# Forward substitution over two 32-token blocks in place of a 64-token block inverse, in a delta-rule attention and gated-convolution kernel

## The chip, the cores and the metric

The kernel runs on one core of one Trainium2 chip. The metric is the time of one execution on the device in microseconds (us); a lower time is better. Engines are named as in the profile: TensorE (PE, with its weight loads as PEld), VectorE (DVE), ScalarE (ACT), GpSimd (POOL) and the queue that issues the transfers (SP).

## The reference, cut to what matters

```
# q, k, v: (4 batches, 8 heads, 768 tokens, 48), beta: (4, 8, 768), all float32
k_n = k / (norm(k) + 1e-6)
state = 0                                  # (4, 8, 48, 48)
for t in range(768):
    y[t]  = q[t] @ state                   # read before the update
    v_old = k_n[t] @ state
    state = state + beta[t] * outer(k_n[t], v[t] - v_old)
x = y, heads side by side                  # (4, 768, 384)
gate_pre[t] = sum over j < 5 of conv_w[j] * x[t - 4 + j]   # per channel
out = (sigmoid(gate_pre) * (x @ w_val)) @ w_out
```

The weights w_val, conv_w and w_out arrive as 64-bit floats and are converted on the chip. All products are float32; in the trace each float32 matmul appears as two MATMUL records and two weight loads.

## The kernel before, in words

The 768 tokens are cut into 12 chunks of 64; a chunk is two blocks of T = 32 tokens. Two chunks make a group, so there are 6 groups. A "unit" is one batch and head; there are 32, worked side by side in the four 32-partition strips and along the free axis.

**prep(g)**, once a group, needs no state. `gram` multiplies keys by keys and by queries (k k' and k q'), `gk` (ScalarE) copies the key part out of PSUM to GD, and `ga` (VectorE, L494) masks the query part into AQ. On VectorE `trans_in` (L523) transposes the 32 by 32 diagonal blocks, `coef` (17 small steps) finds the norms, and then each 32 by 32 triangular block is inverted: `row` (L564, L566) makes 8 by 8 inverses, `mergez8` and `merget8` (L580 to L595) make 16 by 16 ones, `zmul`, `zred`, `tmul`, `tred` (L599 to L619) make 32 by 32 ones. The result is transposed twice, `trans_t` (L623) and `trans_n` (L626). In group 0 alone (FAST) the last merge is made by TensorE instead (`p1`, `p2`, `p3`, with copies). Then `bd0`, `lev1`, `zevac`, `lev2`, `tevac` join the two 32-token inverses of a chunk to one 64-token inverse BD: `lev1` (L686) and `lev2` (L697) are 32 by 32 products on TensorE, with narrow copies by ScalarE. `vscale` (ScalarE) scales the values by the norms.

**chain(c)**, once a chunk, is the serial part: `estep` (keys times state, L801), `esum` (VectorE, L805, subtracts the values), `ustep` (BD times that, L812), `uevac` (three ScalarE copies to US), `sstep` (adds to the state in PSUM, L822), `sevac` (copies it out for the next chunk). `qstep` (L833) and `ystep` (L841) make the output, `flip` (L851) transposes it.

**moe(c)** is the gated convolution: `conv` (L892) makes the first nt taps of the convolution with TensorE, `tap` (L898) the other 5 - nt with VectorE, `sig` (ScalarE), `val` (L907), `gate` (L910), `outp` (L915), `oevac`. nt is 2 for chunks 0 to 5 and 1 for 6 to 11.

Loads go through one queue, each held back until the second load before it has landed. The order of all instructions is made when the kernel is built: a planner simulates the five engines with listed costs, ranks and biases, takes the highest rank among what is ready, chooses the PSUM bank, and puts in `keep_warm` matmuls on zeros (L958) where TensorE would stand idle. Each engine then runs its own list in that order.

Of the kernel before, what the change touches and what calls it, by code (L numbers as in the profile page):

```python
# [21 lines left out]
KW = 5 * T  # L22
# [4 lines left out]
BIAS = {  # L27
    'LB': -1138.3, ('LB', 0): 7.4, 'LK0': 530.9, ('LK0', 0): -481.0, 'LKQ': 1110.0, ('LKQ', 0): -19.7,
    ('LKQ', 1): 156.3, ('LKQ', 2): 217.7, ('LKQ', 3): -442.9, ('LKQ', 4): -892.6, ('LKQ', 5): -89.1, 'LKT': -576.7,
    ('LKT', 0): -196.1, ('LKT', 1): -334.4, ('LKT', 2): 445.2, ('LKT', 3): -254.0, ('LKT', 4): 323.2,  # L30
# [4 lines left out]
    'coef': 468.0, ('coef', 0): 263.6, ('coef', 1): -4.1, ('coef', 2): -237.8, ('coef', 3): -109.9, ('coef', 4): 84.2,  # L35
    ('coef', 5): -151.7, 'const': 613.2, ('const', 0): 1209.5, 'conv': 28.7, ('conv', 0): -1.9, ('conv', 1): -155.4,
    ('conv', 2): 135.3, ('conv', 3): 335.1, ('conv', 4): -180.2, ('conv', 5): 605.0, 'cscale': -43.3,
    ('cscale', 0): -117.7, ('cscale', 1): -746.4, ('cscale', 2): -14.6, ('cscale', 3): 116.5, ('cscale', 4): 29.6,
    ('cscale', 5): -381.6, 'diag': 1076.5, ('diag', 0): -1247.6, 'estep': -7.9, ('estep', 0): 288.5,
    ('estep', 1): -5.2, ('estep', 2): -41.9, ('estep', 3): 734.0, ('estep', 4): 74.9, ('estep', 5): -89.3,  # L40
    'esum': -83.1, ('esum', 0): -380.5, ('esum', 1): -432.1, ('esum', 2): 323.2, ('esum', 3): 833.7,
    ('esum', 4): 122.3, ('esum', 5): 282.5, 'eye': -40.5, ('eye', 0): -581.3, 'f64_bits': 179.7,
    ('f64_bits', 0): -110.7, 'f64_join': -266.8, ('f64_join', 0): -364.4, 'f64_low': 270.2, ('f64_low', 0): 791.0,
    'flip': 208.0, ('flip', 0): 127.2, ('flip', 1): -93.2, ('flip', 2): 82.9, ('flip', 3): 292.3, ('flip', 4): -243.4,
    ('flip', 5): 174.0, 'ga': 126.9, 'gate': -104.8, ('gate', 0): -759.9, ('gate', 1): 509.6, ('gate', 2): -463.4,
# [3 lines left out]
    ('gramK', 0): 128.0, 'gramQ': 430.1, ('gramQ', 0): -160.4, ('gram', 1): -704.8, ('gram', 2): -104.0,  # L49
    ('gram', 3): -4.8, ('gram', 4): 563.1, ('gram', 5): 99.1, 'halo': 185.7, ('halo', 0): -312.1, ('halo', 1): -20.4,  # L50
    ('halo', 2): 245.9, ('halo', 3): -202.4, ('halo', 4): 460.8, ('halo', 5): -382.3, 'high': 162.3, 'lev1': 80.3,
# [6 lines left out]
    ('norm', 1): 328.3, ('norm', 2): -366.6, ('norm', 3): 266.0, ('norm', 4): 610.1, ('norm', 5): -506.2,  # L58
    'oevac': -1050.8, ('oevac', 0): -639.5, ('oevac', 1): 223.7, ('oevac', 2): -293.3, ('oevac', 3): -491.9,
    ('oevac', 4): 428.8, ('oevac', 5): 997.7, 'ones': -1017.8, ('ones', 0): -412.1, 'outp': 254.2,  # L60
    ('outp', 0): -290.2, ('outp', 1): -378.5, ('outp', 2): 246.7, ('outp', 3): 155.7, ('outp', 4): 185.1,
    ('outp', 5): 238.1, 'p1': -8.9, ('p1', 0): -189.4, 'p2': -61.8, 'p2evac': -59.9, ('p2evac', 0): 440.8,
    ('p2', 0): -32.9, 'p3': 33.8, 'p3evac': 482.3, ('p3evac', 0): 751.7, ('p3', 0): -185.1, 'pack': -348.7,
    ('pack', 0): 465.1, 'qstep': 59.2, ('qstep', 0): 391.9, ('qstep', 1): 424.1, ('qstep', 2): -186.8,
    ('qstep', 3): -217.3, ('qstep', 4): -80.2, ('qstep', 5): -107.5, 'row': -870.9, ('row', 0): 33.6,
    ('row', 1): -118.1, ('row', 2): -337.1, ('row', 3): 162.6, ('row', 4): 31.4, ('row', 5): -725.8, 'sevac': 686.4,
    ('sevac', 0): 379.9, ('sevac', 1): -1074.3, ('sevac', 2): 1019.5, ('sevac', 3): 811.9, ('sevac', 4): 1118.8,
    ('sevac', 5): -215.4, 'sig': -419.1, ('sig', 0): 468.8, ('sig', 1): -444.3, ('sig', 2): 787.5, ('sig', 3): -763.0,
    ('sig', 4): 169.1, ('sig', 5): 290.8, 'small': 629.3, ('small', 0): 122.8, 'split': -143.9, ('split', 0): 337.1,
# [944 lines left out]
```

## Time and profile before

| | |
|---|---|
| median of 3 runs | 339.22 us (338.83 to 339.41) |
| profiled execution, span | 340.4 us, mean granted TensorE clock 0.910 |
| TensorE busy | 294.2 us (86%), weight loads 236.6 us |
| VectorE busy | 265.4 us (78%) |
| ScalarE busy | 195.9 us (58%) |
| GpSimd busy | 17.6 us (5%) |
| TensorE matmul records | 8370, 214 of them keep_warm |
| moved by transfers | 34.58 MB |

The profiled execution gives no time beside its span; the span is 1.2 us above the median of the runs. Busy times say how much of the span an engine had an instruction in flight. Records of small matmuls overlap, so what a product costs TensorE is read from start to start in the timeline, not from the mean duration of a record.

### The profile page before, as it was taken

What the parts mean: (1) busy time and instruction counts of PE and PEld (TensorE: products, weight loads), DVE (VectorE), ACT (ScalarE), POOL (GpSimd) and SP (SyncE); (2) the same over time, 40 slices, a digit from 0 to 9 for tenths busy, and PEclk for the clock granted to TensorE, in tenths of its full rate; (3) what the DMA queues carried; (4) which work ended last, traced back from release to release, by engine and by line L of the source; (5) the groups of instructions that cost most, each with busy time, mean ns of one, the idle gap of its engine ahead of it and who ended that gap; (6) DMA issues with size and microseconds to landing.
All of it is one profiled execution on the core that took longest, in us unless ns stands there. A gap on an engine that the chain in (4) does not pass through costs nothing.

```text
span 340.4 us, 18482 instructions
## 1 busy us (share of the span) xinstructions
PE 294.2 (86%) x8370; PEld 236.6 (70%) x8370; DVE 265.4 (78%) x655; ACT 195.9 (58%) x569; POOL 17.6 (5%) x31
## 2 busy tenths in 40 slices
PE   5898544977859898988996997998999999999994
PEld 4797544876647776875875885877866787687862
DVE  5569869895257999998999866999999899827430
ACT  4211759999545965357955478616599351873321
POOL 0000022322200000000000000000000000000000
PEclk9589855969678999999999589999999999999999
DMA  4885666131612527060147104345221301300213
GB/s 149 271 251 155 193 187 187 52 91 58 202 53 81 171 54 233 19 196 11 50 81 257 58 4 157 62 125 162 58 65 26 98 4 25 73 4 2 49 23 69
DMA packets 12379, 34.58 MB, mean 102 GB/s; under 512 B 1933, under 2 KB 5133, under 8 KB 12301
## 3 DMA queue, kind: packets, MB, share of 16 engines
q1 hardware_dynamic: 12300, 33.41, 33.4%
q8 instruction: 65, 1.06, 1.3%
q14 instruction: 14, 0.11, 0.1%
HBM read 28.69 MB, written 4.72 MB: 98 GB/s over the span
## 4 chain that ended last, share of the span: by engine, by line
PE 45%; DVE 21%; ACT 15%; issue 10%; DMA 7%; SPq 0%; POOL 0%; DVEq 0%; ACTq 0%
PE PB L907 8%; PE SPS L958 6%; PE PB L915 5%; PE PB L892 5%; ACT VN L348 5%; PE PB L484 5%; DMA KQ<-in_kq_dram 5%; DVE GT L898 4%; PE PB L801 2%; ACT BD L348 2%; PE PB L833 2%; DVE ZT L606 2%; ACT US L348 2%; DVE PR L599 2%; PE PB L851 2%
## 5 line engine op out<-in xcount | busy, mean ns | idle before, releaser
L907 PE MATMUL PB<-X,WV 128*128 128x256 f32 x216 | 52.5, 388 | 1.5 <-DVE GT L910 1.0
L915 PE MATMUL PB<-WO,GT 128*128 128x384 f32 x144 | 50.6, 495 | 0.1
L348 ACT ACTIVATE VN<-VN,NRM 128x48 f32<-128x48 f32 x192 | 45.1, 326 | 2.2 <-DMA PACE<-VN 2.0
L907 PEld LDWEIGHTS PB<-X,WV 128*128 128x128 f32 x216 | 39.8, 191 | 8.5 <-DVE GT L910 1.2
L898 DVE SCALAR_TENSOR_TENSOR GT<-X,CW,GT 128x256 f32<-128x256 f32 x90 | 38.7, 478 | 0.1
L958 PE MATMUL SPS<-ZW 128*128 128x128 f32 x214 | 35.1, 319 | 3.0 <-DVE SPS L400 2.8
L915 PEld LDWEIGHTS PB<-WO,GT 128*128 128x128 f32 x144 | 26.3, 190 | 15.5 <-DVE GT L910 0.3
L484 PE MATMUL PB<-KQ 48*32 48x96 f32 (+2 forms) x1536 | 26.6, 263 | 11.7 <-issue 9.2
L958 PEld LDWEIGHTS SPS<-ZW 128*128 128x128 f32 x214 | 31.2, 224 | 4.4 <-DVE SPS L400 2.8
L484 PEld LDWEIGHTS PB<-KQ 48*32 48x32 f32 x1536 | 21.3, 113 | 16.0 <-issue 11.9
L892 PE MATMUL PB<-X,CD 128*128 128x256 f32 x108 | 32.0, 432 | 0.1
L348 ACT ACTIVATE OS<-PB 128x384 f32<-128x384 f32 x24 | 11.6, 487 | 34.4 <-PE PB L915 33.1
L910 DVE TENSOR_TENSOR GT<-PB,GT 128x256 f32<-128x256 f32 x36 | 14.9, 417 | 20.5 <-PE PB L907 20.5
L494 DVE TENSOR_TENSOR AQ<-PB,MASK 128x256 f32<-128x256 f32 x48 | 19.2, 418 | 12.7 <-ACT GD L348 12.6
L898 DVE SCALAR_TENSOR_TENSOR GT<-X,CW,PB 128x256 f32<-128x256 f32 x36 | 16.6, 475 | 13.8 <-PE PB L892 8.7
L348 ACT ACTIVATE US<-PB 64x384 f32<-64x384 f32 (+1 forms) x36 | 17.5, 486 | 16.8 <-PE PB L812 9.2
L348 ACT ACTIVATE GD<-PB 128x256 f32<-128x256 f32 x48 | 15.6, 381 | 18.8 <-PE PB L484 18.4
L348 ACT ACTIVATE BD<-PB 32x256 f32<-32x256 f32 (+1 forms) x50 | 19.1, 383 | 8.7 <-PE PB L697 5.8
L892 PEld LDWEIGHTS PB<-X,CD 128*128 128x128 f32 x108 | 21.0, 210 | 3.6 <-DVE GT L898 0.3
L902 ACT ACTIVATE GT<-GT 128x256 f32<-128x256 f32 x36 | 13.6, 413 | 15.3 <-DVE GT L898 15.2
L841 PEld LDWEIGHTS PB<-US,AQ 64*64 64x64 f32 x768 | 14.3, 146 | 9.7 <-ACT US L348 7.1
L348 ACT ACTIVATE ZS<-PB 32x256 f32<-32x256 f32 x48 | 17.9, 373 | 4.1 <-PE PB L686 3.1
(117 smaller groups left out, 481.9 us busy)
## 6 DMA issues: line engine op xcount, KB each, us to landing
KQ<-in_kq_dram SPq DMA_DIRECT2D x24, 640.0 KB, 5.0
VN<-in_vt_dram SPq DMA_DIRECT2D x12, 384.0 KB, 3.5
KT<-in_kt_dram SPq DMA_DIRECT2D x12, 384.0 KB, 3.2
out_dram<-OS SPq DMA_DIRECT2D x48, 96.0 KB, 2.2
BD<-in_k_dram SPq DMA_DIRECT2D x2, 512.0 KB
OS<-in_w_val_dram SPq DMA_DIRECT2D x2, 384.0 KB, 4.0
GT<-in_w_out_dram SPq DMA_DIRECT2D x2, 384.0 KB
PACE<-KQ SPq DMA_DIRECT2D x24, 0.0 KB
```

The source lines that it names most:

```text
L348: A.activation(out=out, in_=in_, func=AF.Copy, **kw)
L484: PE.matmul(o, w, y, start=True, stop=True, tile_position=(64 * r, q))
L494: V.tensor_tensor(out=AQ[c % NAQ][:, r, 4 * i:4 * i + 4, :].rearrange("p h (n t) -> p h n t", t=T), in0=gview(c, i, r, part)[:, :, 0:3:2, ...
L599: V.tensor_tensor(out=PR[:, 0:64 * n].rearrange("p (k i j) -> p k i j", k=4, i=16), op=ALU.mult, in0=tl4[:, 1, :, 0, 4 * kb:16].unsqueeze( ...
L841: PE.matmul(bank("y", c, r)[a:a + C, D * h:D * h + D], aq[64 * t:64 * t + C, r, h, :], us[64 * t:64 * t + C, r, h, :], start=c == 0 and h ...
L892: PE.matmul(p, CD[:, m, k], x[:, m, :, k:k + C], start=(k == 0), stop=(k == nt - 1))
L898: V.scalar_tensor_tensor(out=GT[m], in0=x[:, m, :, k:k + C], scalar=CW[:, m, k:k + 1], in1=csum(m) if k == nt else GT[m], op0=ALU.mult, op ...
L902: A.activation(out=GT[m], in_=csum(m) if nt == KS else GT[m], func=AF.Sigmoid)
L907: PE.matmul(p, WV[:, k, 128 * m:128 * m + 128], xs[:, k], start=(k == 0), stop=(k == NKX - 1))
L910: V.tensor_tensor(out=GT[m], in0=bank("v", c, m)[:, 0:B * C].rearrange("p (b t) -> p b t", t=C), in1=GT[m], op=ALU.mult)
L915: PE.matmul(bank("o", c, i)[:, 0:DM], GT[k][:, 2 * i:2 * i + 2, :].rearrange("p b t -> p (b t)"), WO[:, k, :], start=(k == 0), stop=(k == ...
L958: PE.matmul(SPS[0][:, 384:512], ZW, ZW, start=False, stop=True, skip_group_check=True)
```

## The change: what it does

The 64-token inverse is no longer built. BD keeps only the 32 by 32 inverses (in another layout, read with a stride), and the chain solves the chunk in two steps: `ustep(0)` applies the inverse to the first block, two copies bring the result out, `ucross` multiplies it by the key products between the two blocks and adds that onto what `estep` left in PSUM for the second block, `esum(1)`, `ustep(1)` and two more copies finish it. `estep` is issued as 64 matmuls of 32 columns instead of 32 of 64. `lev1`, `lev2`, `bd0`, `zevac`, `tevac` and `trans_n` go.

FAST is empty: group 0 uses VectorE's `zmul` to `tred` as the others do, and `p1` to `p3` are never called. `gram` becomes one 64 by 128 product per unit (32 matmuls per chunk instead of 64); in groups 1 to 5 GpSimd then puts the blocks in place (`gmove`, 4 copies of 32 partitions a chunk). In group 0 keys are multiplied first (`gram0`), half of the copies out are VectorE's (`gkv`). `coef` has 15 steps instead of 17. GpSimd also copies norms (`nswap`) and does one step of the weight conversion. The convolution taps on TensorE become 3 for chunks 0 to 3, 1 for 4 to 7 and 0 for 8 to 11. Keys and queries are loaded as two tensors without the copies that were in `kq`: a half chunk has 512 KB instead of 640 KB, and the separate key load of group 0 is the first half itself. PSUM banks are cleared at the start by VectorE and ScalarE. The planner is gone: ORDER lists the number of each operation in the order of issue (-1 is a `keep_warm`), and SLOTS the PSUM banks.

```diff
+WG = 544
+FAST = ()
+NTAP = [3, 3, 3, 3, 1, 1, 1, 1, 0, 0, 0, 0]
+F64P = (1,)
+ORDER = [
+    13, 12, 20, 1, 0, 2, 3, -1, 5, -1, 4, 14, 6, 17, 15, 135, 21, 18, 19, 16, 301, 24, 8, 22, 23, 300, -1, 25, 26,
...
+]
...
+    V.memset(SPS[0], 0.0)
+    for i in range(NBANK):
+        if i < 3:
+            V.memset(PB[i], 0.0)
+        else:
+            copy(PB[i], ZW[:, 0:1].to_broadcast([128, 512]))
...
 def gram(c, i, part):
+            for r, t in STREAMS:
+                rows = slice(64 * r, 64 * r + D)
+                w = x[rows, 0, t ^ r, h, :]
+                o = bank("g", c, i, r, part)[64 * t:64 * t + C]
...
+                    PE.matmul(o[:, 2 * C * j:2 * C * j + 2 * C].rearrange("p (n e) -> p n e", e=C), w, x[rows, :, t ^ r, h, :],
+                              start=True, stop=True, tile_position=(64 * r, 64 * t))
...
+    def gmove(c, r, t):
+        u = unit(c // 2, c, r)[64 * t + T * (1 - r):64 * t + T * (1 - r) + T].rearrange("p h (n e) -> p h n e", e=T)
+        G.tensor_copy(out=u[:, :, r], in_=u[:, :, 1 - r])
...
+        def trans_t(i):
+            V.transpose(out=BD[gb][:, 16 * i:16 * i + 16], in_=tf[:, :, 16 * i:16 * i + 16].rearrange("p k j -> p j k"))
...
         def estep():
             for h in range(H):
+                for s in range(2):
+                    for r, t in STREAMS:
+                        q = 64 * t + T * s
+                        PE.matmul(bank("e", c, r ^ s)[q:q + T, D * h:D * h + D], x[64 * r:64 * r + D, 0, t ^ r, h, T * s:T * s + T],
+                                  sp[64 * r:64 * r + D, t ^ r, h, :], start=h == 0, stop=not s ^ r, skip_group_check=True,
+                                  tile_position=(64 * r, q))
+        def ustep(n):
+            for h in range(H):
                 for r, t in STREAMS:
+                    q = 64 * t + T * (r ^ n)
+                    PE.matmul(bank("u", c, r)[q:q + T, D * h:D * h + D], bd[q:q + T, :, u0 + 8 * r + h],
+                              (E2 if n else E1 if c else vn[:, 0])[q:q + T, h, :], start=True, stop=True, tile_position=(q, q))
+        def ucross():
+            for h in range(H):
+                for r, t in STREAMS:
+                    q, to = 64 * t + T * r, 64 * t + T * (1 - r)
+                    PE.matmul(bank("e", c, 1)[to:to + T, D * h:D * h + D], unit(g, c, r)[q:q + T, h, T * (1 - r):T * (1 - r) + T],
+                              us[q:q + T, r, h, :], start=c == 0 and h == 0, stop=True, skip_group_check=True, tile_position=(q, to))
...
+        add("PE", ustep, (0,), w=both("up"), take=both("u"), r=["E1" if c else ("VN", 0, 0), ("BD", g % 2, c % 2)])
+        for r in range(2):
+            add("ACT", uevac, (r,), r=[("up", c, r)], w=[("U", c % 2, r)])
+        add("PE", ucross, r=Ur + GDL, w=[("ep", c, 1)], take=() if c else [("e", c, 1)])
+        add("DVE", esum, (1,), r=[("ep", c, 1)] + VS[1], w=["E2"], give=[("e", c, 1)])
+        add("PE", ustep, (1,), w=both("up"), r=["E2", "q", ("BD", g % 2, c % 2)])
```

Numbering the operations as the changed file adds them gives 1,528. Read with that numbering, ORDER has 159 `keep_warm` entries, 153 of them ahead of chunk 2's `estep`; it puts 99 VectorE instructions from group 0's first `trans_in` up to chunk 0's `ustep(0)` and 178 up to chunk 2's `estep`; between that `estep` and the last `trans_t` of group 5 it has 405 VectorE instructions, and behind that point TensorE has, as the bulk, 7 `outp` and 9 `val`. In the stretches around a chain it puts one `val`, `outp` or `conv` between `ustep(0)` and `ucross`, and mostly one between `ucross` and `ustep(1)`.

## Rows read from the trace of the kernel before

**Rows 1.** Four stretches: busy time of each engine (instructions), clock, DMA.
```profile
0.00:66.70 66.70, 47.00 (x1760) 42.95 (x1760) 51.66 (x166) 34.80 (x103) 7.51 (x14) 0.77 0.60 181
66.70:106.20 39.50, 30.37 (x1123) 25.60 (x1122) 21.93 (x45) 27.18 (x76) 7.31 (x9) 0.74 0.30 93
106.20:291.00 184.80, 172.63 (x4654) 134.47 (x4653) 170.59 (x397) 113.14 (x341) 2.54 (x8) 0.97 0.32 93
291.00:341.00 50.00, 44.19 (x846) 33.61 (x844) 21.18 (x49) 20.78 (x50) 0.22 (x1) 1.00 0.15 34
```

**Rows 2.** Timeline of TensorE: start, length, count of records.
```profile
66.66 1.61 PE L812 MATMUL PB<-VN,BD 64*64 64x48 f32 x64
...
106.16 1.15 PE L801 MATMUL PB<-ST,KQ 48*64 48x48 f32 x64
```

**Rows 3.** Timeline of VectorE: start, length.
```profile
9.93 1.91 DVE L523 STREAM_TRANSPOSE TLP<-GD 128x1024 f32<-128x1024 f32 x1 [3.24 <-ACT GD L348]
...
57.27 1.58 DVE L599 TENSOR_TENSOR PR<-TLP,TT__78 128x768 f32<-128x768 f32 x1
...
289.02 2.22 DVE L623 STREAM_TRANSPOSE BD<-TT__78 128x1024 f32<-128x1024 f32 x1
```

**Rows 4.** VectorE by line, 106.2 to 341 us: count, busy us, mean ns.
```profile
L898 DVE SCALAR_TENSOR_TENSOR GT<-X,CW,GT 128x256 f32<-128x256 f32 x87 | 37.2, 478 | 0.0
...
L612 DVE TENSOR_TENSOR PR<-ZT,TR 128x256 f32<-128x256 f32 (+3 forms) x16 | 13.1, 821 | 0.3
...
L606 DVE TENSOR_REDUCE ZT<-PR 128x64 f32<-128x1024 f32 (+3 forms) x16 | 13.0, 814 | 0.3
...
L494 DVE TENSOR_TENSOR AQ<-PB,MASK 128x256 f32<-128x256 f32 x24 | 9.7, 420 | 0.3 <-ACT GD L348 0.3
L623 DVE STREAM_TRANSPOSE BD<-TT__78 128x1024 f32<-128x1024 f32 x4 | 8.9, 2218 | 0.0
L626 DVE STREAM_TRANSPOSE TNA<-TT__78 128x1024 f32<-128x1024 f32 x4 | 7.9, 1969 | 0.0
L564 DVE TENSOR_TENSOR PR<-TT__78,TLP 128x16 f32<-128x16 f32 (+5 forms) x24 | 6.1, 254 | 0.7
...
L580 DVE TENSOR_TENSOR PR<-TLP,TT__78 128x256 f32<-128x256 f32 (+1 forms) x16 | 5.0, 354 | 0.2
...
L584 DVE TENSOR_REDUCE ZT<-PR 128x64 f32<-128x512 f32 (+1 forms) x8 | 4.4, 553 | 0.3
...
L536 DVE SCALAR_TENSOR_TENSOR QUOT<-QUOT,SQ 128x32 f32<-128x32 f32 x10 | 1.9, 189 | 0.1
```

**Rows 5.** One weight-conversion step, whole trace by form.
```profile
L429 DVE TENSOR_SCALAR GT<-GT 128x384 uint32<-128x384 uint32 x3 | 1.1, 354 | 0.0
```

**Rows 6.** Timeline of TensorE from 213.9 us, full clock.
```profile
213.90 1.88 PE L484 MATMUL PB<-KQ 48*32 48x96 f32 x128
215.70 2.86 PE L907 MATMUL PB<-X,WV 128*128 128x256 f32 x12
218.49 0.94 PE L822 MATMUL SPS<-US,KT 64*48 64x48 f32 x64
219.36 0.87 PE L851 MATMUL PB<-EYE,YS 128*128 128x128 f32 x6
220.07 2.10 PE L915 MATMUL PB<-WO,GT 128*128 128x384 f32 x6
222.10 1.15 PE L801 MATMUL PB<-ST,KQ 48*64 48x48 f32 x64
223.18 1.56 PE L892 MATMUL PB<-X,CD 128*128 128x256 f32 x6
```

**Rows 7.** Timeline of TensorE: a 32 by 32 product.
```profile
244.71 1.31 PE L686 MATMUL PB<-BD,GD 32*32 32x32 f32 x128
```

**Rows 8.** ScalarE by line and form: one copy of the chain.
```profile
L348 ACT ACTIVATE US<-PB 128x384 f32<-128x384 f32 x12 | 5.9, 489 | 16.3 <-PE PB L812 9.2 <-DVE GT L898 7.0
```

**Rows 9.** Timeline of GpSimd: two weight joins of one size.
```profile
57.04 0.99 POOL L441 TENSOR_TENSOR WV<-WV,GT 128x384 f32<-128x384 f32 x1 [11.40 <-ACT WV L437]
58.11 1.59 POOL L442 TENSOR_TENSOR WV<-WV,GT 128x384 f32<-128x384 f32 x1
```

More of the change, by code (lines that the diff above doesn't have):

```diff
@@ L1 @@
-import math
 from contextlib import ExitStack
@@ L141, in add @@
             self.bank[key] = n
+            self.slot[key] = len(self.slot)
         for key in give:
             first = self.bank[key]
[L144 to L145 removed]
+            self.ops[first][3].update(d for d in deps if d < first)
+        self.ops.append((eng, fn, args, deps, tuple(take), tuple(give)))
         self.kinds.append((kind or fn.__name__, self.part))
@@ L263, with where @@
+        seen = set()
+        for n in ORDER:
+            if n >= 0:
+                assert self.ops[n][3] <= seen
+                seen.add(n)
+        assert len(seen) == len(self.ops)
+        return ORDER
+    def where(self, key):
+        return SLOTS[self.slot[key]]
 @with_exitstack
@@ L713, in plan_gram @@
             for i in range(2):
                 gg = [("g", c, i, r, part) for r in range(2)]
-                add("PE", cost, gram, (c, i, part), cols=cols, size=128, r=use, w=[("gp", c, i, r, part) for r in range(2)],
-                    take=gg, kind="gram" + part)
+                gp = [("gp", c, i, r, part) for r in range(2)]
+                if part == "K":
+                    add("PE", gram0, (c, i), r=[K], w=gp, take=gg)
+                else:
+                    add("PE", gram, (c, i, part), r=[K, ("KQ", c % NKQ, 1)], w=gp, take=gg, kind="gram" + part)
@@ new lines, in prep @@
+        for i in range(2):
+            add("DVE", trans_in, (i,), r=GDT[0] + GDT[1], w=[("TL", i)])
+        TLs = [("TL", i) for i in range(2)]
+        for step in range(15):
+            add("DVE", coef, (step,), r=TLs if step == 0 else ["BE"] if step == 14 else [],
+                w=["CF"] + (["CT"] if step == 14 else []), kind="coefr" if step == 13 else "coef")
+        add("DVE", norm, r=["CF"], w=[("NRM", gb)])
+        for q in range(0, 128, 32):
+            for n in ((0, 1) if q % 64 else (None,)):
+                add("POOL", nswap, (q, n), r=[("NRM", gb)], w=[("NRN", gb, q, n)])
@@ L858, in chain @@
         if c:
-            add("PE", 1.05, estep, cols=938, size=128, r=KQr + Sr, w=both("ep"), take=both("e"))
-            for r in range(2):
-                add("DVE", 0.49, esum, (r,), r=[("ep", c, r), ("VN", c % NKT, r)], w=[("ES", r)], give=[("e", c, r)])
-        if c:
-            add("PE", 1.08, qstep, cols=938, size=128, r=KQr + Sr, w=both("yp") + ["q"], take=both("y"))
-        add("PE", 1.05, ustep, cols=1086, size=128, w=both("up"), take=both("u"),
-            r=([("ES", r) for r in range(2)] if c else [("VN", c % NKT, r) for r in range(2)])
-            + [("BD", g % 2, c % 2, z) for z in "LH"] + [("BD", g % 2, c % 2, q, n) for q, n in QN] + ["q"])
@@ L867, in chain @@
-        for r, t in ((0, 0), (1, 0), (1, 64)):
-            add("ACT", 0.42, uevac, (r, t), r=[("up", c, r)], w=[("U", c % 2, r, t)], give=[("u", c, r)] if r == 0 or t else ())
-        Ur = [("U", c % 2, r, t) for r, t in ((0, 0), (1, 0), (1, 64))]
+            add("PE", estep, r=KQr[:1] + Sr, w=both("ep"), take=both("e"))
+            add("DVE", esum, (0,), r=[("ep", c, 0)] + VS[0], w=["E1"], give=[("e", c, 0)])
+            add("PE", qstep, r=KQr[1:] + Sr, w=both("yp") + ["q"], take=both("y"))
@@ L870, in chain @@
+        for r in range(2):
+            add("ACT", uevac, (r,), r=[("up", c, r)], w=[("U", c % 2, r)], give=[("u", c, r)])
         if not last:
-            add("PE", 0.83, sstep, cols=814, size=128, r=[("KT", c % NKT)] + Ur, w=["sp0", "sp1"])
+            add("PE", sstep, r=[("KT", c % NKT)] + Ur, w=["sp0", "sp1"])
             for a in range(2):
-                add("ACT", 0.42, sevac, (a,), r=[f"sp{a}"], w=[("S", (c + 1) % 2, a)])
-        add("PE", 1.03, ystep, cols=1086, size=128, w=both("yp"), take=() if c else both("y"),
+                add("ACT", sevac, (a,), r=[f"sp{a}"], w=[("S", (c + 1) % 2, a)])
@@ L928, in moe @@
             for k in range(nt, KS):
-                add("DVE", 0.4, tap, (m, k), r=X_ + [("Xh", c % 3), "CW"] + ([("cp", c, m)] if k == nt else []), w=[gt],
-                    give=[("c", c, m)] if k == nt else ())
-            add("ACT", 0.36, sig, (m,), r=[("cp", c, m)] if nt == KS else [], w=[gt], give=[("c", c, m)] if nt == KS else ())
-            add("PE", 1.42, val, (m,), cols=1536, r=X_ + [("W", i) for i in range(1, NKX + 1)], w=[("vp", c, m)],
-                take=[("v", c, m)], size=12)
@@ L934, in moe @@
-            add("DVE", 0.34, gate, (m,), r=[("vp", c, m)], w=[gt], give=[("v", c, m)])
+                add("DVE", tap, (m, k), r=X_ + [("Xh", c % 3), "CW"] + ([("cp", c, m)] if k == nt and nt else []), w=[gt],
+                    give=[("c", c, m)] if k == nt and nt else ())
+            add("ACT", sig, (m,), r=[("cp", c, m)] if nt == KS else [], w=[gt], give=[("c", c, m)] if nt == KS else ())
+            add("PE", val, (m,), r=X_ + [("W", i) for i in range(1, NKX + 1)], w=[("vp", c, m)], take=[("v", c, m)])
@@ L947 @@
+    add("SP", load, (BE, beta), w=["BE"], kind="LB")
     for g in range(NG):
```

711 lines of the change are left out of this document (252 added, 459 removed), and 96 rows, old and new, of tables (BIAS, ORDER, SLOTS).

## The prediction

> **What bounds the kernel now.** I read the four stretches first, then the timelines of the two busiest engines, then the prices.
>
> In the stretches the reader is to see three regimes [rows 1]. Up to chunk 2's `estep` at 106.2 us [rows 2] TensorE runs at a clock of 0.74 to 0.77, and much of its 47.0 us busy up to 66.7 is `keep_warm`; it waits for chunk 0's `ustep`, which begins at 66.7 us [rows 2]. VectorE, with 51.7 of 66.7 us, is busiest: the prep of groups 0 and 1 is a serial string there that begins at 9.9 us [rows 3]. From 106.2 to 291, where group 5's `trans_t` ends (289.0 plus 2.2 us) [rows 3], both engines are nearly full: TensorE 172.6 and VectorE 170.6 of 184.8 us [rows 1]. Behind 291 only TensorE is: 44.2 us busy of the 49.4 that are left, VectorE 21.2 [rows 1]. So the time is the sum of three stages with three limits: the start (VectorE and the waits of group 0), the middle (both engines), the tail (TensorE). ScalarE has room throughout, 113.1 of 184.8 us in the middle [rows 1]; what the change takes from it I cost at nothing. I work out the new time stage by stage and make the sum against the span, 340.4 us; the runs' median is 1.2 us below that, so 1.2 comes off at the end. A measurement of this kernel tells about 0.2% (0.7 us) from no change.
>
> **The start.** Now the 34 us before chunk 0's `ustep` go through `p1` to `p3`, `lev1`, `lev2` and eight rounds of copies. The change replaces all that by VectorE's own merge and one transposition. VectorE then sets the pace, so I add up the 178 instructions that ORDER gives it from group 0's first `trans_in` to chunk 2's `estep`:
>
> - 32 of the last merge, 16 multiplies at 0.821 and 16 sums at 0.814 us (two groups of rows like these two): 26.2 [rows 4]
> - 24 of the merge to 16: 16 at 0.354, 8 at 0.553: 10.1 [rows 4]
> - 26 `row` steps at 0.254: 6.6; 30 `coef` steps at 0.189: 5.7; 23 `ga` at 0.420: 9.7 [rows 4]
> - 4 halves of `trans_in` at half of 1.91: 3.8 [rows 3]; 4 halves of `trans_t` at half of 2.218: 4.4 [rows 4]
> - 21 steps of weight conversion at 0.354: 7.4 [rows 5]
> - 14 others (norms, scales, `esum`, two taps) between a `coef` step and a tap of 0.478 us [rows 4]: an estimate of 5
>
> The sum is 78.9 us. Neighbours overlap a little when they don't depend on each other: 87 taps of 0.478 are 41.6 us and took 37.2, a ratio of 0.89, while 16 sums of the merge took all of their 13.0 [rows 4]. The string is mostly dependent, so I take 0.97: 76.5 us. K arrives and `gram0` has the same 64 matmuls a chunk as now, so the string begins where it does now, at 9.9 us, and chunk 2's `estep` comes at 86.4; with a little waiting, 87 us in place of 106.2. The bounds are 80 (0.89, no waiting) and 94 (1.0 and 5 us of waiting, a third of the 15 us that VectorE idles now before 66.7 [rows 1]). The first 99 of these instructions by the same prices are 42 us, which puts chunk 0's `ustep(0)` near 51. `keep_warm` grows from 107 to 159 matmuls, nearly all in this stage, where TensorE waits anyhow: nothing. PSUM clearing is four more VectorE writes ahead of 9.9 us, where VectorE waited 3.2 us for the key copies [rows 3]: nothing.
>
> **The middle, TensorE.** Prices from start to start at full clock [rows 6]: `gram` takes 1.80 us for 128 records, `val` 1.40 for 6, `sstep` 0.87 for 64, two `flip` 0.71 for 6, `outp` 2.03 for 6, `estep` 1.08 for 64; `ustep` now has `estep`'s 64 tiles of this size, so also 1.08. `lev1` takes 1.31 for the 128 records of a group, 10.2 ns each [rows 7], and `lev2` has as many; that is 1.31 per chunk for the two. A chunk loses `gram`, `lev1` and `lev2`, `estep`, `ustep`: 1.80 + 1.31 + 1.08 + 1.08 = 5.27 us. It gains:
>
> - `estep` as 128 records 32 columns wide, and `ustep(0)`, `ucross`, `ustep(1)` as 192 records of 32 by 32 with 48 columns moving. The trace has no such product. Below stands `lev1`'s 10.2 ns, same tile with 32 columns moving; above stands `estep`'s 1.08/64 = 17 ns, 64 wide with the same 48. I take 11.5, near `lev1`, since the tile is the same: 1.47 + 2.21.
> - `gram` as 64 records of 64 by 64 with 128 columns moving. A whole-array record with 128 columns (`flip`) takes 0.71/6 = 118 ns [rows 6]; four tiles side by side would make it 30, two 59, and `sstep`'s 0.87/64 = 14 ns is the floor. I take 30, since the present `gram`, at 14 ns for 96 columns on tiles half as wide, also runs about that far side by side: 1.92.
>
> That is 5.60, or 0.33 more per chunk, some 3 us over the stage. The convolution puts about as many matmuls into this stage as now (3 taps for the early chunks, none for the last). TensorE comes to about 176 us.
>
> **The middle, VectorE.** ORDER gives it 405 instructions against 397 [rows 1]. Taps, gates and merges are equal in number to within one. `trans_n` goes (three inside this stage at 1.97 us: -5.9 [rows 4]), a half `trans_in`, a `ga` and a few `coef` steps come. I make it 4 us less, 166.5.
>
> So neither engine's load moves enough to be seen, and both stay above 90% of the stage. I keep 184.8 us. The bounds are 178 (TensorE's 176 with hardly a gap) and 195 (the longer chain, below, uncovered for about a third). GpSimd's `gmove` and `nswap` ride on an engine that is busy 2.5 of 184.8 us [rows 1], a group ahead of need: nothing, but see the last rival. Transfers shrink (24 halves of 512 in place of 640 KB); SP's queue loses the two key loads and gains none: nothing.
>
> **The tail.** Behind group 5's `trans_t` TensorE has 7 `outp` at 2.03, 9 `val` at 1.40, of chunk 10 three small products (2.21), `sstep` 0.87, `ystep` 1.08 (priced as `estep`), `flip` 0.71, and of chunk 11 1.47 + 1.08 + 2.21 + 1.08 + 0.71 [rows 6]: 38.3 us. With the 5.2 that are not busy now (49.4 - 44.2) [rows 1] it is 43.5, 6 less than now: the last chunks' convolution has gone to VectorE, which has 21.2 of 49.4 us to do there now.
>
> **The sum**: 87 + 184.8 + 43.5 = 315.3 us of span, 25 less; as a median of runs 314.
>
> **The rivals.**
>
> *The chain is no longer covered (slower).* Each chunk's chain grows by `ucross` 0.74, an `esum` of about 0.5, `ustep(1)` 0.74 and two copies at 0.489 [rows 8]: 3.0 us, 36 over 12 chunks, with one more round trip through ScalarE and VectorE. Behind the waiting matmuls all of TensorE's list queues. Uncovered, it gives 314 + 36 = 350. It decides against the change from 25/12 = 2.1 us per chunk, two thirds of the addition. Against it: a `val`, `outp` or `conv` (1.4 to 2.0 us) stands in the list between the steps, and a copy pair needs 1.0; and a chunk has 184.8/8 = 23 us. For it: VectorE is full in the middle, so `esum(1)` can come late behind a merge step of up to 1.2 us.
>
> *The small products cost 17 ns, not 11.5.* Then 5.5 ns times 320 records times 11 chunks add 19 us to a TensorE that has no room: 333. The tile speaks against it, the 48 moving columns for it.
>
> *Both engines pack better.* The start at its lower bound (80) and the middle at 178, with a tail of 43.5, give 301.5, as a median 300. For it: the present list has stalls that need not be there, such as a mean clock of 0.97 in the middle [rows 1]. Against it: VectorE is at 92% already.
>
> *GpSimd slows VectorE.* While a GpSimd join ran from 57.0 to 59.7 us, VectorE's multiply of 768 elements took 1.58 us, where the four sizes of this step (640 elements on average) take 0.82 on average [rows 4], so that about 1.0 was due; and the second of two equal joins took 1.59 against 0.99 [rows 3, 9]: each may cost the other 0.6. The 32 `gmove` in the middle, half of them meeting such a multiply, are 10 us on VectorE: 324. The Trainium skill, "GPSIMD Engine Reference", section 1 Specifications, says that GpSimd shares VectorE's access to SBUF and that instructions of VectorE with two SBUF inputs contend with it. By that rule the time would be this rival's; the pair of rows agrees that there is such a loss, but shows it once.
>
> **How the numbers follow.** The forecast, 314 (305 to 325 by itself), has 0.55; better packing 0.15; the dearer products 0.12; the uncovered chain 0.10; GpSimd 0.08. The range runs from 299 (packing) to 336 (dearer products with the late start) and leaves out the uncovered chain and a little below: some 0.15. Faster by over 0.2%: the forecast, packing, GpSimd and most of the dearer products, 0.86; slower 0.11; the same 0.03.
>
> **What the new profile would show.** Chunk 0's `ustep(0)` near 51 and chunk 2's `estep` near 87 us, with VectorE almost without gaps before; else the start is wrong. From there to group 5's last `trans_t` about 185 us with both engines over 90%; waits of TensorE on copies to US or on `esum` above 2 us a chunk would be the uncovered chain. Records of `ustep` 11 to 12 ns apart, `gram` 1.9 us a chunk; no `lev1`, `lev2`. A tail of 43 to 44 us. The prediction is wrong if TensorE's list was made for other costs than the chip's, so that it waits in the middle although its load is the same.

## The result, and the profile after

The changed kernel takes 313.85 us (median of 4 runs, 312.28 to 315.56) against 339.32 us for the kernel before on the same chip: a ratio of 0.925, 95% interval 0.920 to 0.930. The profiled execution after has a span of 310.5 us (its time is 312.28, the shortest of its runs); between the two profiled spans lie 29.9 us, between the medians 25.5. Here and below, medians are of all runs of a kernel, while ratios and intervals leave out runs more than 1.5% above its fastest.

The same four stretches as in [rows 1], cut at the same events (chunk 0's first `ustep`, chunk 2's `estep`, the end of group 5's `trans_t`); columns as there:

```profile
0.00:49.60 49.60, 44.54 (x769) 41.75 (x769) 45.58 (x125) 15.51 (x44) 16.56 (x30) 1.00 0.51 160
49.60:88.10 38.50, 31.41 (x1037) 27.68 (x1037) 36.29 (x83) 24.61 (x74) 19.34 (x24) 0.91 0.37 120
88.10:261.80 173.70, 170.67 (x5058) 134.86 (x5058) 163.16 (x407) 90.49 (x288) 20.49 (x59) 1.00 0.30 89
261.80:311.00 49.20, 42.83 (x896) 31.62 (x895) 24.02 (x59) 16.17 (x40) 0.44 (x2) 0.97 0.20 47
```

The events themselves, and the new products, in the timeline of TensorE after (four stretches of it):

```profile
49.57 1.55 PE L732 MATMUL PB<-VN,BD 32*32 32x48 f32 x64 [0.37 <-DVE BD L570]
...
88.12 1.42 PE L721 MATMUL PB<-ST,KQ 48*32 48x48 f32 x128
89.47 1.57 PE L821 MATMUL PB<-X,CD 128*128 128x256 f32 x6
...
161.06 1.98 PE L389 MATMUL PB<-KQ 48*64 48x128 f32 x64
162.86 0.90 PE L748 MATMUL SPS<-US,KT 64*48 64x48 f32 x64
...
172.83 1.13 PE L732 MATMUL PB<-E,BD 32*32 32x48 f32 x64
173.90 2.20 PE L847 MATMUL PB<-WO,GT 128*128 128x384 f32 x6
176.03 0.88 PE L739 MATMUL PB<-US,GD 32*32 32x48 f32 x64
176.84 0.70 PE L821 MATMUL PB<-X,CD 128*128 128x256 f32 x2
```

The start (to chunk 2's `estep`) is 18 us shorter than in [rows 2], the middle 173.7 us in place of 184.8, and the tail about as long as before (48.7 us and 49.4). From start to start, `estep` takes 1.35 us, `gram` 1.80, `ustep` 1.07, `ucross` 0.81.

The middle is where the reader should look twice. TensorE was idle for 184.80 - 172.63 = 12.2 us of it before and for 173.70 - 170.67 = 3.0 us now: 9.1 of the 11.1 us. What it waited for most in the middle before (waits of TensorE: waiting line, releaser, us in total, times, longest):

```profile
PE PB L484 <- issue: 4.0, 3, 1.4
PE PB L841 <- ACT US L348: 2.2, 3, 1.1
PE PB L484 <- DMA KQ<-in_kq_dram: 1.3, 2, 0.9
PE PB L697 <- issue: 1.3, 2, 0.9
PE SPS L822 <- issue: 1.1, 1, 1.1
PE PB L907 <- DVE GT L910: 1.0, 1, 1.0
PE PB L812 <- issue: 0.3, 1, 0.3
```

And all that this view lists of the middle after:

```profile
PE PB L759 <- issue: 1.4, 1, 1.4
PE PB L732 <- issue: 0.7, 1, 0.7
PE PB L767 <- issue: 0.2, 1, 0.2
```

"Issue" is time in which TensorE waited for nothing that the profile shows: 6.7 us before, 2.3 now. Most of it was at L484, `gram`, and `gram` now has half as many records. The other waits, on copies, a transfer and VectorE, were 5.5 us before and are under 1 now.

### The profile page after: what moved, and what is told of

It reads as the page before. It is cut to its first block, busy times and chain, and to the rows that moved or that the text cites. A ratio compares the mean times of both kernels' runs of the same rounds, so it can differ in the third digit from the quotient of the medians.

```text
span 310.5 us, 17236 instructions
## 1 busy us (share of the span) xinstructions
PE 289.5 (93%) x7758; PEld 235.9 (76%) x7758; DVE 269.1 (87%) x669; ACT 146.8 (47%) x446; POOL 56.8 (18%) x114
## 4 chain that ended last, share of the span: by engine, by line
PE 74%; DVE 17%; issue 3%; ACT 2%; POOL 2%; DMA 1%; POOLq 0%; ACTq 0%
PE PB L839 16%; PE PB L847 16%; PE PB L821 7%; PE PB L732 7%; PE PB L389 5%; PE PB L721 4%; PE SPS L887 4%; PE PB L759 3%; PE PB L767 3%; PE PB L739 3%; PE PB L777 3%; DVE PR L559 2%; PE SPS L748 2%; DVE PR L546 2%; DVE ZT L553 2%
## 5 line engine op out<-in xcount | busy, mean ns | idle before, releaser
L250 ACT ACTIVATE VN<-VN,NRN 128x48 f32<-128x48 f32 x176 | 49.4, 330 | 1.2 <-POOL NRN L484 1.2
L250 ACT ACTIVATE US<-PB 128x384 f32<-128x384 f32 x48 | 21.5, 487 | 56.7 <-PE PB L732 53.5
L887 PEld LDWEIGHTS SPS<-ZW 128*128 128x128 f32 x318 | 41.0, 208 | 3.3 <-DVE SPS L268 1.7
L422 POOL COPY GD<-GD 32x256 f32<-32x256 f32 x40 | 19.3, 483 | 59.1 <-ACT GD L250 29.2
L732 PEld LDWEIGHTS PB<-E,BD 32*32 32x32 f32 x1472 | 23.6, 145 | 8.1 <-issue 3.0
L732 PE MATMUL PB<-E,BD 32*32 32x48 f32 x1472 | 26.7, 218 | 1.4 <-DVE E L726 0.8
L842 DVE TENSOR_TENSOR GT<-PB,GT 128x256 f32<-128x256 f32 x36 | 15.0, 420 | 12.2 <-PE PB L839 11.9
L389 PE MATMUL PB<-KQ 48*64 48x128 f32 x640 | 21.7, 273 | 2.2 <-issue 2.0
L250 ACT ACTIVATE OS<-PB 128x384 f32<-128x384 f32 x24 | 11.5, 487 | 23.9 <-PE PB L847 23.9
L389 PEld LDWEIGHTS PB<-KQ 48*64 48x64 f32 x640 | 17.8, 133 | 4.6 <-issue 2.5
L559 DVE TENSOR_TENSOR PR<-ZT,TR 128x256 f32<-128x256 f32 (+3 forms) x24 | 20.6, 859 | 0.1
L546 DVE TENSOR_TENSOR PR<-TLP,TT__78 128x1024 f32<-128x1024 f32 (+3 forms) x24 | 20.0, 835 | 0.1
```

The costliest lines, as they stand in the source:

```text
L250: A.activation(out=out, in_=in_, func=AF.Copy, **kw)
L389: PE.matmul(o[:, 2 * C * j:2 * C * j + 2 * C].rearrange("p (n e) -> p n e", e=C), w, x[rows, :, t ^ r, h, :], start=True, stop=True, tile_ ...
L422: G.tensor_copy(out=u[:, :, r], in_=u[:, :, 1 - r])
L546: V.tensor_tensor(out=PR[:, 0:64 * n].rearrange("p (k i j) -> p k i j", k=4, i=16), op=ALU.mult, in0=tl4[:, 1, :, 0, 4 * kb:16].unsqueeze( ...
L559: V.tensor_tensor(out=PR[:, 0:64 * n].rearrange("p (k i j) -> p k i j", k=16, i=4), op=ALU.mult, in0=z16[:, :, 0:n].unsqueeze(2).to_broadc ...
L732: PE.matmul(bank("u", c, r)[q:q + T, D * h:D * h + D], bd[q:q + T, :, u0 + 8 * r + h], (E2 if n else E1 if c else vn[:, 0])[q:q + T, h, :] ...
```

## The experiments

Times are medians; the changed kernel's 313.85 us (ratio 0.925) is what each is held against, unless it says otherwise. The kernel before gave 339.3 to 342.0 us beside these runs, so a difference under some 3 us is not told from none.

**The operations or the order list.** Two kernels, neither with a tuned list: the kernel before with an empty table BIAS, and the changed kernel's operations put in order by that same planner.

```
-BIAS = {'LB': -1138.3, ...}
+BIAS = {}
```

Expected of the first:

> The kernel before, its planner's table of per-kind offsets (BIAS) emptied, so that its order list is the planner's first draft; products unchanged. It is one half of a pair with e2. How far the draft is from the tuned list the trace cannot say: an estimate of 340 to 370 us. If the change's gain is its operations (my theory), e2 is some 25 us (15 to 35) below this run; if the gain is the new order list and the operations are worth nothing (rival), e2 and this run agree within 5 us.

Expected of the second:

> The changed kernel's operations, put in order not by the list written out but by the planner of the kernel before, with its table of offsets emptied and prices of the same kind as there. Operations are worth the gain (my theory): some 25 us (15 to 35) below e1, and chunk 0's first ustep begins about 15 us earlier than in e1. The list is worth the gain (rival): within 5 us of e1. Both share it: in between, and the distance of this run from 313.9 us is what the list is worth.

Measured 383.6 us (ratio 1.133, interval 1.126 to 1.141) and 376.2 us (1.109, 1.100 to 1.118). Chunk 0's first `ustep` and chunk 2's `estep` on TensorE's timeline of the first:

```profile
66.74 1.30 PE L742 MATMUL PB<-VN,BD 64*64 64x48 f32 x37
...
107.03 1.96 PE L731 MATMUL PB<-ST,KQ 48*64 48x48 f32 x64
```

And of the second:

```profile
53.45 1.13 PE L788 MATMUL PB<-VN,BD 32*32 32x48 f32 x64 [0.30 <-DVE BD L626]
...
94.09 0.84 PE L777 MATMUL PB<-ST,KQ 48*32 48x48 f32 x68
```

Neither theory holds whole. The start's gain comes with the operations, under a poor list too: 13.3 us at chunk 0's `ustep` and 12.9 at chunk 2's `estep`, of 17.1 and 18.0 in the tuned pair. Behind the start the new operations under the plain list lose some 5 us again. TensorE's "issue" waits over the whole execution are 30.6 us in the first and 18.6 in the second, and 29.5 and 8.4 in the tuned pair: the operations bring them down, and so does the list. And a tuned list is worth 44 us to the old operations and 62 to the new: the gain of 25 is there only because both kernels have a list fitted to them.

**Where `ustep` got its price.** BD stored unit by unit, so that a weight is 32 adjacent numbers:

```
-    BD = tiles(2, [128, T, NU], "BD")
+    BD = tiles(2, [128, NU, T], "BD")
...
-  PE.matmul(..., bd[q:q + T, :, u0 + 8 * r + h], ...
+  PE.matmul(..., bd[q:q + T, u0 + 8 * r + h, :], ...
```

> The changed kernel with BD stored unit by unit, so that ustep's weights are read as 32 adjacent numbers instead of 32 numbers 128 bytes apart; trans_t writes with that stride instead. The stride makes ustep dear (theory): its 64 records fall from 1.07 to about 0.81 us like ucross, 23 usteps save 6 us of TensorE, and as TensorE is busy 98% of the middle, most of it shows: 308 to 311 us, if trans_t costs no more than now. What makes ustep dear is not the stride but that it reads VectorE's sums in it (rival): ustep stays at 1.07 and the time at 314.

Measured 313.4 us (308.8 to 316.0; ratio 0.917, interval 0.906 to 0.928). Weight loads of `ustep` and the transposition, by line (records, busy us, mean ns), in the changed kernel:

```profile
L732 PEld LDWEIGHTS PB<-E,BD 32*32 32x32 f32 x1472 | 23.6, 145 | 8.1 <-issue 3.0 <-DVE GT L830 1.2 <-DVE E L726 1.0
...
L570 DVE STREAM_TRANSPOSE BD<-TT__78 128x512 f32<-128x512 f32 x12 | 12.8, 1066 | 0.0
```

And with BD by units:

```profile
L732 PEld LDWEIGHTS PB<-E,BD 32*32 32x32 f32 x1472 | 17.5, 105 | 8.7 <-issue 3.9 <-DVE E L726 1.6 <-DVE GT L830 0.7
...
L570 DVE STREAM_TRANSPOSE BD<-TT__78 128x512 f32<-128x512 f32 x12 | 13.8, 1148 | 0.0
```

The stride is the price: a load falls from 145 to 105 ns, and TensorE's share in these products by 6 us; VectorE pays 1.0 us of it back. In time nothing is shown: two runs took 308.8 and 311.8 us, two 315.0 and 316.0, and the interval overlaps that of the changed kernel (0.920 to 0.930). The middle was 171.6 us, 2.1 shorter, and the start 2.1 longer in the profiled execution, in which the clock from 76 to 91 us was 0.89 and not 1.00. I took it to mean that VectorE sets the middle.

**Which engine sets the middle.** Three kernels that leave work out: the value product without its third block of features, the convolution without its last tap, and both.

```
-            for k in range(NKX):
+            for k in range(NKX - 1):
                 PE.matmul(p, WV[:, k, ...], xs[:, k], ...
...
         def tap(m, k):
+            if k == KS - 1:
+                return
```

> The changed kernel with the value product summed over two of its three blocks of features (k = 0, 1), so 36 val of 0.93 instead of 1.40 us: TensorE loses 16.8 us, 12.1 of it in the middle and 4.2 in the tail (26 and 9 val). VectorE sets the middle (theory after the run with BD stored by rows, where TensorE lost 6 us and the end did not move): only the tail's share shows, 308 to 311 us. TensorE sets the middle (its 98% busy, rival): 297 to 301 us.

> The changed kernel without the last tap (k = 4) of the convolution: 36 VectorE instructions of about 0.477 us less, 17 us, of it some 26, 12.4 us, in the middle. VectorE sets the middle: 301 to 306 us (TensorE's 170.7 us busy there stop it after 3 us if that figure is real work, in which case 309 to 311). TensorE sets it: 312 to 314 us.

> Both together: 36 val over two blocks, and no last tap. VectorE alone sets the middle: as without the tap alone, less the tail's 4 us. TensorE alone: as with the shorter val alone. Both do, each the other's limit (third theory): more is saved than in the two runs together, 295 to 300 us.

Measured 301.9 us (ratio 0.886, interval 0.880 to 0.893), 314.5 (0.926, 0.918 to 0.934) and 300.1 (0.883, 0.876 to 0.889). The middle of the first, by the same events:

```profile
88.80:255.80 167.00, 162.58 (x5017) 126.23 (x5017) 161.04 (x406) 90.89 (x289) 19.62 (x58) 1.00 0.31 92
```

Of the second:

```profile
88.90:263.30 174.40, 169.99 (x5059) 134.19 (x5058) 154.38 (x379) 90.48 (x288) 18.86 (x56) 1.00 0.30 89
```

And of the third:

```profile
87.50:255.50 168.00, 161.69 (x5017) 125.72 (x5016) 155.03 (x381) 90.69 (x290) 19.98 (x59) 1.00 0.31 92
```

My second theory falls. VectorE loses 8.8 us of work in the middle and the middle does not move; TensorE loses 8.1 and it is 6.7 shorter; taking both away adds nothing that can be told. VectorE, 94% busy, has room; TensorE sets the middle.

**The chain.** Both copies of the first half of U issued twice:

```
-        def uevac(r):
-            copy(us[:, r], vw(bank("u", c, r)))
+        def uevac(r, n=1):
+            for _ in range(n):
+                copy(us[:, r], vw(bank("u", c, r)))
...
-            add("ACT", uevac, (r,), ...
+            add("ACT", uevac, (r, 2 if c else 1), ...
```

> The changed kernel with both copies of the first half of U issued twice in chunks 1 to 11: about 1.0 us more between ustep(0) and ucross, on ScalarE and on the chain. The chain is covered by other products in TensorE's list (my theory): 313 to 317 us, 0 to 3 more. It is not covered (rival of the prediction): about 11 more, 325 us.

Measured 318.9 us (ratio 0.937, interval 0.929 to 0.944): 5 of the 11 us show, nearly half. The middle is 5.9 us longer, and a wait stands in it that was not there, `ucross` for the copies (waits of TensorE, middle):

```profile
PE PB L739 <- ACT US L250: 2.8, 5, 1.0
```

That is half of the 5.9 us. "Issue" waits grew by as much, from 2.3 to 5.1 us, though the records are the same in number. So the chain's cover is thin: as the kernel stands nothing waits for these copies, and of the one microsecond tried in each chunk about half came through.

**Records.** Each `gram` matmul cut in two, so that `gram` has 128 records a chunk again:

```
-  PE.matmul(o[:, 2 * C * j:2 * C * j + 2 * C].rearrange(...), w, x[rows, :, t ^ r, h, :], ...
+  for n in range(2):
+      PE.matmul(o[:, 2 * C * j + C * n:2 * C * j + C * n + C], w, x[rows, n, t ^ r, h, :], ...
```

> The changed kernel with each gram matmul cut in two, the 64 key columns and the 64 query columns, on the same weights and into the same places: 128 records a chunk in place of 64, as the kernel before had, the same columns in all. The fewer records are why TensorE no longer stops for its instructions in the middle (there 6.7 us of issue waits before, 4.0 of them at gram; 2.3 after): some 4 to 8 us slower, with issue waits at gram of 1 us and more in most chunks, 318 to 322 us. The order list, not the records, did away with these waits (rival): 313 to 315 us, unless 128 records of 64 columns themselves cost more than 64 of 128 columns, which the mean spacing at gram shows.

Measured 332.1 us (ratio 0.981, interval 0.973 to 0.989): 18 us slower, two and more times what I expected. The middle, by the same events:

```profile
90.80:280.30 189.50, 176.64 (x5445) 139.58 (x5445) 161.93 (x405) 91.09 (x288) 17.42 (x56) 0.98 0.28 82
```

All waits of TensorE in it:

```profile
PE PB L390 <- issue: 3.8, 5, 1.4
PE PB L722 <- issue: 3.2, 2, 2.0
PE PB L733 <- issue: 2.9, 2, 2.3
PE PB L760 <- issue: 1.2, 1, 1.2
PE PB L768 <- issue: 1.1, 1, 1.1
```

And two of the stops, on its timeline:

```profile
126.52 2.02 PE L390 MATMUL PB<-KQ 48*64 48x64 f32 x116 [0.70 <-issue]
128.47 0.30 PE L722 MATMUL PB<-ST,KQ 48*32 48x48 f32 x12
129.98 1.26 PE L722 MATMUL PB<-ST,KQ 48*32 48x48 f32 x116 [1.20 <-issue]
```

The middle grew by 15.8 us: 6.0 of busy time and 9.9 of waits (12.2 against 2.3), all of them "issue". They stand at `gram` (L390) and also behind it, at `estep` (L722) and `ustep` (L733), whose code is the same. Of the busy time 3.7 us are `gram` itself (16.4 against 12.7); and around a stop of 2.0 us that ended at 155.1 us the granted clock fell to 0.51 until 161.1, where an `outp` took 4.0 us in place of 2.0. Between the two stops 128 matmul records run, 116 of `gram` and 12 of `estep`, in 3.46 us. That number is no accident. In the timelines of all fourteen kernels here TensorE has 210 "issue" stops over 0.15 us, and from one to the next it runs 128 records or a multiple of that, but for a few records that the traces lack (in the kernel before, the stops that end at 44.50, 48.88, 53.15 and 57.43 us are 128 apart each). So these stops come only at every 128th record. In this middle it stopped at eleven such places; before nine of the eleven the 128 records had run through in under 3 us, and only one stretch without a stop had been that fast. So the stops go with short records in close ranks; the list was fitted to half as many at `gram`.

**A version from what was found.** BD by units, and the one tap that TensorE has in chunks 4 to 7 given to VectorE:

```
+        shift = 4 <= c < 8
+
         def conv(m):
+            if shift:
+                return
...
+            if shift and k == nt:
+                V.tensor_scalar(out=GT[m], in0=x[:, m, :, 0:C], scalar1=CW[:, m, 0:1], ...
```

> The changed kernel with BD stored by rows and, in chunks 4 to 7, the one tap of the convolution that TensorE has (12 conv of about 0.47 us) given to VectorE (12 more of 0.348 us). TensorE loses 6 + 5.6 us, VectorE gains 4 + 1. TensorE sets the middle and VectorE has room (what the shorter val, with half of its saving there kept, and the left-out tap, with none, show): half of it and the tail's share, 306 to 310 us. VectorE's string decides: 314 to 318 us.

Measured 310.07 us (6 runs, 308.8 to 313.6; ratio 0.915, interval 0.908 to 0.922), the lowest median of the kernels that leave nothing out. The intervals of the two kernels just overlap, so a gain of about 1% is likely, not certain. TensorE's busy time in the middle fell by 7.2 us and the middle only by 1.6, to 172.1, in which VectorE is now busy 166.9 (its window, columns as above):

```profile
89.30:261.40 172.10, 163.50 (x5045) 126.91 (x5045) 166.93 (x419) 90.94 (x289) 20.54 (x60) 1.00 0.30 90
```

The longest wait of TensorE in it:

```profile
PE PB L732 <- DVE E L726: 3.1, 2, 1.7
```

`ustep` now waits for VectorE's sums: moving work across uses up the room that VectorE had.

**The share of the convolution by itself**, given to the kernel before:

```
-PTAP = {6: 1, 7: 1, 8: 1, 9: 1, 10: 1, 11: 1}
+PTAP = dict(enumerate([3, 3, 3, 3, 1, 1, 1, 1, 0, 0, 0, 0]))
```

> The kernel before with the new share of the convolution (3 taps on TensorE in chunks 0 to 3, 1 in 4 to 7, none in 8 to 11, in place of 2 and 1), ordered anew by its planner. The share of the taps is worth little by itself (my theory; the tail's 6 us at most): 333 to 342 us. It is what shortens the tail and the middle (rival): 325 us or less.

Measured 355.3 us (ratio 1.048, interval 1.038 to 1.058): slower, against both expectations. Its planner's offsets were fitted to the old shares, so the run tells little of the shares; that they bring the gain by themselves it does not bear out.

**GpSimd.** `gmove` on ScalarE, and `gmove` issued twice:

```
 def gmove(c, r, t):
-    G.tensor_copy(out=u[:, :, r], in_=u[:, :, 1 - r])
+    copy(u[:, :, r], u[:, :, 1 - r])
```

```
 def gmove(c, r, t):
-    G.tensor_copy(out=u[:, :, r], in_=u[:, :, 1 - r])
+    for _ in range(2):
+        G.tensor_copy(out=u[:, :, r], in_=u[:, :, 1 - r])
```

> The changed kernel with gmove's 40 copies on ScalarE instead of GpSimd. GpSimd slows VectorE (rival of the prediction, at its price of 0.6 us for each of the about half that meet a two-input instruction: 10 us): 304 to 308 us. They cost VectorE little because they seldom meet one (my theory): 312 to 315 us, ScalarE having room; ScalarE's copies could delay an evacuation by 0.3 us each, under 2 us in all.

> The changed kernel with every gmove issued twice: 40 more copies of about 0.48 us on GpSimd, 19 us, nearly all with VectorE at work beside them. GpSimd slows VectorE (rival of the prediction, 0.6 us for each of the half of them that meets a two-input instruction): some 12 more, 326 us, and VectorE's instructions at the same place are longer. The loss is small (theory, after the run with gmove on ScalarE, where chunk 0's first ustep came 0.8 us earlier): 0 to 3 more, 314 to 317 us.

Measured 320.0 us (ratio 0.945, interval 0.935 to 0.954) and 322.1 us (0.943, 0.934 to 0.952). Both are slower, by 6 to 7 us going by the ratios, and for neither of the two reasons on offer. VectorE's busy time is the same: 269.1 us in the changed kernel, 269.6 with twice the `gmove`. That is not because a copy slows nothing, but because few copies meet an instruction that they slow. Of the 40 `gmove` in the changed kernel ten run beside a VectorE instruction with both inputs in SBUF; of the nine such instructions four are 0.09 to 0.22 us longer than the same ones elsewhere, 0.7 us in all. With the copies doubled it is 20 of 80, and five of 16 instructions by 0.06 to 0.19 us, 0.9 us in all. One case in the changed kernel, the four copies and a multiply whose five likes take 0.68 us:

```profile
76.08 2.06 POOL L422 COPY GD<-GD 32x256 f32<-32x256 f32 x4 [0.30 <-ACT GD L250]
76.54 0.90 DVE L559 TENSOR_TENSOR PR<-ZT,TR 128x512 f32<-128x512 f32 x1
```

`ga`, which reads one input from PSUM, takes 415 ns on average in both kernels. What is new is a wait, here VectorE's longest with the doubled copies (the next group's `trans_in`, for `gmove`):

```profile
DVE TLP L448 <- POOL GD L423: 7.1, 4, 2.4
```

With the copies on ScalarE the same instruction waits for that engine, and `ga` stands in its queue too:

```profile
DVE AQ L417 <- ACT GD L250: 4.2, 5, 2.4
DVE TLP L447 <- ACT GD L250: 3.6, 4, 1.6
```

`gmove` is thus on the path to the next group's prep, with little slack: the doubling adds eight copies of 0.48 us, 3.9 us, to each of five groups, and before four of them `trans_in` waited, 7.1 us in all.

## Why the prediction was right, and where its steps were not

- **The start: right.** Forecast 51 and 87 us for chunk 0's `ustep` and chunk 2's `estep`; they came at 49.57 and 88.12, with VectorE busy 45.58 and 36.29 us of the 49.6 and 38.5. From the first `trans_in`, at 10.6 us, to that `estep` VectorE was busy 74.2 us of 77.5, where my sum had 76.5. The untuned pair shows that this part belongs to the operations. What I did not see is that TensorE's stops stood in the old path: in the 20 us of `p1` to `p3`, 37.8 to 58.1 us, 12.0 are "issue" waits (L646, L659 and L671). How much of the 17 us gained they are was not tried.

```profile
PE PB L646 <- issue: 4.9, 1, 4.9
PE PB L659 <- issue: 4.8, 2, 2.4
PE PB L671 <- issue: 2.3, 1, 2.3
```

- **`gram` and `estep`: right.** 1.80 us against 1.92, and 1.35 against 1.47.
- **The small products: the size was off for one.** `ucross` took 0.81 us, 12.7 ns a record against 11.5. `ustep` took 1.07, 16.7 ns, the rival's price: not for its 48 columns, which `ucross` has too, but for weights read 128 bytes apart. That is 0.33 us on each of 16 `ustep`, 5.3 us in the middle that I did not have. (`lev1`, my floor, I took at its length; from start to start it is 1.24 us, 9.7 ns a record.)
- **The middle: the step that failed** is "so neither engine's load moves enough to be seen ... I keep 184.8 us". It kept the idle time, the filler and the clock of the old list as if they belonged to the load. It was 173.7, under my lower bound of 178: here the rival "both engines pack better" came, which I had put at 0.15. The bound had its reason right, TensorE with hardly a gap; its load was 170.7 and not 176. In part an `outp` and a `qstep` (3.1 us) fell behind the boundary, and `keep_warm`, which I had counted as load, went from 34 records and 6.7 us to 6 and 1.3. In part it is the clock. Before, TensorE was busy for only 2.3 of the 5.1 us up to 187.3; then the granted clock was 0.50 (1.2 GHz) until 197.4, and an `estep` there took 1.88 us from start to start in place of 1.08. By that ratio some 4 of these 10.1 us, an estimate, are the lower clock's. The changed kernel has the full clock (2.4 GHz) in all of its middle. The stretch before, and its `estep`:

```profile
187.30:197.40 10.10, 10.10 (x229) 8.80 (x229) 7.28 (x13) 5.52 (x14) 0.22 (x1) 0.50 0.16 47
188.02 1.96 PE L801 MATMUL PB<-ST,KQ 48*64 48x48 f32 x64
```

Of the 9.1 us less of idle time 4.4 are "issue" waits. Splitting `gram` alone brought 9.9 us of such waits, so the one `gram` product, which my sum had as 0.12 us a chunk dearer, has a part in this. It is not the number of short records: a chunk had 384 of them in `gram`, `lev1`, `lev2`, `estep` and `ustep`, and it has 384 in `gram`, `estep`, `ustep` and `ucross` now. It is how closely they follow on each other. I priced records by their spacing while they flow, and not by what the stream can be supplied with. The text of the kernel before has that term: its planner lets TensorE wait at every `BLOCK = 256` of its instructions.
- **The tail: mis-sized.** 48.7 us (310.5 - 261.8) against 43.5: the two products that fell behind the boundary are 3.1 of it, four `ustep` at 0.33 more are 1.3, and of the last 0.8 most is idle time (5.9 us, where I kept 5.2).
- **The sum.** 315.3 against a span of 310.5. The middle came 11.1 us shorter than forecast, the tail 5.2 and the start 1.1 longer; and the median was 3.4 us above that span, where I took 1.2 off. So the closeness of 314 to 313.85 is luck: errors that cancel.
- **The uncovered chain: it did not come, by a small margin.** In the middle no wait on copies to US or on `esum` was left. The lengthened chain shows that one more microsecond per chunk is paid by about half.
- **GpSimd slows VectorE: it does, but `gmove` hardly.** The loss that [rows 3, 9] showed is there in the start, beside the weight joins (below). Beside the `gmove` I had put it at 10 us; it was 0.7, as ten of the 40 copies and not half met such an instruction, and none cost more than 0.22. So the price of a join is not that of a copy. By the rule of the Trainium skill that I weighed ("GPSIMD Engine Reference", section 1 Specifications) VectorE's instructions with two SBUF inputs contend; these runs agree: the slowed instructions have two, and `ga`, with one input in PSUM, takes 0.41 us beside joins and beside copies as elsewhere. And "a group ahead of need: nothing" was wrong of `gmove`: `trans_in` needs its result almost at once.

The loss beside a join, on VectorE's timeline after: a multiply of 4 elements, and the next one, of 16.

```profile
53.09 0.84 DVE L499 TENSOR_TENSOR TT__78<-TT__78,TLP 128x4 f32<-128x4 f32 x1
53.97 0.17 DVE L502 TENSOR_TENSOR PR<-TT__78,TLP 128x16 f32<-128x16 f32 x1
```

The joins on GpSimd's timeline at that time:

```profile
52.86 1.04 POOL L344 TENSOR_TENSOR WV<-WV,OS 128x384 f32<-128x384 f32 x1 [3.31 <-DVE OS L338]
53.98 1.01 POOL L347 TENSOR_TENSOR WV<-WV,OS 128x384 f32<-128x384 f32 x1
```

The small multiply, which takes 0.16 us on average the other five times, lasts until the first join ends; the next one, issued between the two, takes its usual 0.17 us.

What stays open: why the middle's other waits (4.8 us on copies, transfers and VectorE) went, and how much of the stops and of the clock is the new operations' and how much the new list's; neither was tried by itself in the tuned kernel. That the "issue" stops are the fetching of instructions was not measured; shown is that they come only at every 128th matmul record. The Trainium skill, "Runtime: NRT & Kernel Launch", section Instruction fetch mechanics, says that an engine's instructions come in blocks of 256 and that crossing into the next is mostly hidden. By that figure, 128 matmuls with their 128 weight loads would be one block, an estimate that fits the distances of the stops; but what stopped TensorE there was not hidden, 0.7 and 1.2 us in the two shown.

## What to carry to other kernels

Look at how closely the records of short tiled matmuls follow on each other, not only at their time: here the same columns in twice the records cost 18 us, and of the 15.8 of them in the middle 9.9 were stops, some at other products. Before keeping an old stage's length because its load is the same, split that length into work, filler, clock and waits, and ask which of these the new instructions can still have. An engine at 94% may have room while another at 98% has none, and an engine at 18% may hold the path; take some work off one engine at a time to see which.

## What the runs showed of the hardware

- A weight load of 32 columns whose numbers lie 128 bytes apart took 145 ns, and 105 ns with adjacent numbers, in a product otherwise the same.
- From one "issue" stop of TensorE to the next lie 128 matmul records or a multiple of that, in all fourteen traces; one such pair is 3.46 us from end to end. With 64 more records a chunk the stops added 9.9 us to a stage of 174 us.
- After 5.1 us in which TensorE was busy for 2.3, the granted clock was 0.50 for 10.1 us, and an `estep` took 1.88 us in place of 1.08.
- While a two-input GpSimd join of 1.0 us ran, a 4-element multiply of VectorE with both inputs in SBUF took 0.84 us in place of 0.16; GpSimd's one-input copies of 256 elements on 32 partitions made such instructions longer by 0.22 us at most. `ga`, with one input in PSUM, took 0.41 us beside either.
